# Strassen's seven block products in the second layer of a fused attention and MLP kernel

## The chip, the cores and the metric

The kernel runs on one core of one Trainium2 chip. The metric is device time in microseconds (us), measured around the whole launch. The time before is 336.84 us, the median of 3 runs (336.18 to 337.52). All runs in this document are of the same undisturbed state, "fast". In the profile, PE is TensorE's matmul, PEld its weight load, DVE is VectorE, ACT is ScalarE, POOL is GpSimd, SP is SyncE (SPq its sequencer). PSUM is the memory in which the kernel puts TensorE's results, and a bank is one buffer of it. The granted clock is the share of TensorE's full clock in the clock records of the trace.

## The reference

Sliding-window attention (window 64) on 8 batches, 8 heads, 576 tokens and 64 columns per head, then a layer norm and a two-layer MLP with a residual:

```python
scores = scale * q @ k.T;  scores = where(0 <= i - j < 64, scores, -1e9)
x  = softmax(scores) @ v                    # [8, 576, 512]
xn = (x - mean) / sqrt(var + 1e-6) * g_ln
out = x + relu(xn @ w_ch1) @ w_ch2          # w_ch1 [512, 2048], w_ch2 [2048, 512]
```

## The kernel before

The tokens are taken in nine groups of 512: groups 0 to 7 are tokens 0 to 511 of each batch, group 8 is the last 64 tokens of all eight. While TensorE runs the MLP of group g, the attention of group g+1 is woven in. The MLP is a list of units, and `at(i, f, ...)` puts a piece of other work behind unit i. So this list is the program order, for every engine. The code is shortened, and the remarks behind # are added.

```python
def b_step(g, kb):                       # attention of 128 tokens, then the mean and variance
    ...                                  # 16 matmuls, reciprocal, xn, bn_stats, bn_aggr
    nc.vector.scalar_tensor_tensor(      # z = (x - mean) * g: needs no variance
        out=z, in0=xn, scalar=mvg[g][:, kb, 0:1], in1=gB, op0=ALU.subtract, op1=ALU.mult)

def zt_step(g, kb, eng="act"):           # z transposed by TensorE, copied out by ScalarE
    for kc in range(NKC):
        nc.tensor.transpose(out=ztp[:, kc, :], in_=z[:, 128*kc:128*(kc+1)], identity=ident16)
    nc.scalar.copy(out=zT[g][:, :, 128*kb:128*kb+128], in_=ztp)

def l2(kb, part):                        # layer 2: 64 matmuls of 512 columns for a group
    for hc in range(4 * part, 4 * part + 4):
        nc.tensor.matmul(out=ch[kb], lhsT=hrT[:, hc, 128*kb:128*(kb+1)], rhs=w2s[:, hc, :], ...)
    if part == 3: add_out(kb)

def add_out(kb):                         # 1/sigma is applied here, at the very end
    nc.vector.scalar_tensor_tensor(out=o, in0=ch[kb], scalar=rstd[g][:, kb:kb+1],
                                   in1=xn, op0=ALU.mult, op1=ALU.add)
    nc.sync.dma_start(out=out[...], in_=o)

# groups 2 to 7; units 0-15 are layer 1, units 16-31 layer 2
for j in range(4):
    at(1 + 6*j, s_mm, b, j);  at(2 + 6*j, s_mask, b, j)
    at(7 + 6*j, b_step, b, j);  at(min(13 + 6*j, 29), zt_step, b, j)
at(13, group_stats, g)                   # 1/sigma of group g by Newton steps
```

ReLU lets 1/sigma wait until the output, so no matmul waits for a variance.

The softmax here doesn't subtract the row's maximum and nothing guards it: scores larger than these inputs give would overflow.

## Time and profile before

The page of the kernel before, parts 1, 2 and 4. The first line has busy time, share of the span and instructions of each engine. The two strips have one digit (tenths) for each of 40 slices of the span. The last line is the chain of waits that ended last, by engine.

```profile
PE 322.8 (96%) x2887; PEld 171.9 (51%) x2887; DVE 168.0 (50%) x307; ACT 175.5 (52%) x292; POOL 114.8 (34%) x198
...
PE   7988999999999999999999999999999999999994
...
PEclk9999999999999999999999999999999999999999
...
PE 85%; DVE 4%; SPq 4%; DMA 2%; ACT 1%; issue 1%; POOL 1%; ACTq 0%
```

TensorE is busy 96% of the time at full clock (mean granted clock 1.000). VectorE has half its time free, on average.

Windows of the kernel before, for groups 0, 1, 4 and 8. The columns are start:end and length, busy time (and instructions) of PE, PEld, DVE, ACT and POOL, then the granted TensorE clock, DMA share and GB/s.

```profile
20.40:59.50 39.10, 36.97 (x345) 20.80 (x345) 24.46 (x43) 19.11 (x33) 25.26 (x26) 1.00 0.99 308
59.50:98.20 38.70, 37.34 (x426) 26.26 (x425) 27.34 (x49) 22.44 (x36) 15.53 (x27) 1.00 0.58 155
...
167.90:201.90 34.00, 34.00 (x305) 17.53 (x304) 17.16 (x31) 19.46 (x32) 13.77 (x23) 1.00 0.69 169
301.70:334.60 32.90, 27.90 (x129) 12.41 (x127) 4.17 (x8) 9.55 (x16) 1.58 (x8) 1.00 0.16 40
```

In group 4, PE is busy 34.00 of 34.00 us and DVE half of it. In group 1, DVE is already at 27.34 of 38.70.

The timeline of the kernel before, TensorE: two stretches of 8 matmuls of 256 columns (layer 1 of group 1), and two of layer 2 at 512 columns in group 8. The columns are start, duration, engine, line, operation, output and inputs, shapes, and how many.

```profile
63.73 1.04 PE L377 MATMUL hph_0_3_1063<-zT_827,w1g 128*128 128x256 f16 x8
64.60 1.04 PE L377 MATMUL hph_0_4_1073<-zT_827,w1g 128*128 128x256 f16 x8
...
319.07 3.62 PE L353 MATMUL ch_1_4645<-w2s,hrT_4513 128*128 128x512 f16 x16
322.53 1.67 PE L353 MATMUL ch_2_4666<-w2s,hrT_4513 128*128 128x512 f16 x7
```

From start to start, 8 matmuls of 256 columns take 0.87 us, 109 ns each; 16 of 512 take 3.46 us, 216 ns each. Half the columns is half the time, with a new weight for each matmul (a weight load takes 98 ns).

The same view, VectorE and GpSimd, in layer 2 of group 4:

```profile
191.00 1.50 POOL L117 CAST qk_1_6_1_2954<-qk_1_6_1_2754 128x1024 f16<-128x1024 f32 x1
191.53 1.52 DVE L264 TENSOR_TENSOR pt_3_3010<-pt_3_3010,mask 128x1024 f16<-128x1024 f16 x1
```

The mask takes about 0.68 us without a cast beside it, and 1.52 us here; the cast, usually 1.04 us, took 1.50. So both became longer where they met.

### The profile page before, as it was taken

The numbers are of one execution on the slowest core, as the hardware profiler recorded it, in microseconds if no ns is written. First come the engines' busy times: TensorE is split into PE (matmuls) and PEld (weight loads), VectorE is DVE, ScalarE is ACT, GpSimd is POOL, SyncE is SP. The second block draws the span as 40 slices with busy tenths as digits, with TensorE's granted clock in tenths as the row PEclk, the third lists the DMA queues.
The fourth block names the chain that finished last, engine by engine and source line by source line (L and its number), as shares of the span: only waits on it lengthen the run. The fifth ranks groups of instructions, "written<-read, shape, count | busy, mean of one in ns | idle before, by whom it ended". The sixth has DMA issues, their size and how long they took to land.

```text
span 334.6 us, 6996 instructions
## 1 busy us (share of the span) xinstructions
PE 322.8 (96%) x2887; PEld 171.9 (51%) x2887; DVE 168.0 (50%) x307; ACT 175.5 (52%) x292; POOL 114.8 (34%) x198
## 2 busy tenths in 40 slices
PE   7988999999999999999999999999999999999994
PEld 2556445786554455545545554456445444444441
DVE  1795682777933565286415751767235714241011
ACT  2586515485267644974468356763675157505500
POOL 7577655413800195008400780058004103201000
PEclk9999999999999999999999999999999999999999
DMA  8999999976239557950369188903460155020022
GB/s 194 284 385 258 355 265 297 256 232 123 62 105 309 103 104 187 309 103 34 118 212 216 29 199 255 219 23 97 118 104 2 65 149 72 16 82 33 0 63 63
DMA packets 85410, 51.02 MB, mean 152 GB/s; under 512 B 55713, under 2 KB 76193, under 8 KB 85378
## 3 DMA queue, kind: packets, MB, share of 16 engines
q1 hardware_dynamic: 84736, 48.24, 54.1%
q0 software_dynamic: 640, 2.33, 3.1%
q8 instruction: 22, 0.36, 0.5%
q14 instruction: 10, 0.08, 0.1%
q10 hardware_dynamic: 2, 0.00, 0.0%
HBM read 38.80 MB, written 9.44 MB: 144 GB/s over the span
## 4 chain that ended last, share of the span: by engine, by line
PE 85%; DVE 4%; SPq 4%; DMA 2%; ACT 1%; issue 1%; POOL 1%; ACTq 0%
DMA w1s_126<-in_moe_w_ch_dram 2%; SPq L130 2%; SPq L78 1%; PE ch_2_852 L353 1%; PE ch_2_3635 L353 1%; PE ch_1_4056 L353 1%; PE ch_1_3588 L353 1%; PE ch_2_3076 L353 1%; PE ch_2_2587 L353 1%; PE ch_1_1979 L353 1%; PE ch_1_4421 L353 1%; PE ch_2_4077 L353 1%; PE ch_1_3029 L353 1%; PE ch_1_2540 L353 1%; PE ch_2_2026 L353 1%
## 5 line engine op out<-in xcount | busy, mean ns | idle before, releaser
L341 PEld LDWEIGHTS <-w1g 128*128 128x128 f16 x480 | 44.9, 98 | 53.0 <-issue 2.9
L377 PEld LDWEIGHTS <-w1g 128*128 128x128 f16 x192 | 18.1, 98 | 5.4 <-issue 2.1
L454 PE MATMUL warm<-mbias,ident_99 128*128 128x512 f16 x21 | 8.1, 491 | 2.3 <-DVE mbias L434 2.3
L353 PEld LDWEIGHTS <-hrT_4513 128*128 128x128 f16 x64 | 6.3, 98 | 7.5
L353 PEld LDWEIGHTS <-hrT_3733 128*128 128x128 f16 x64 | 6.0, 98 | 7.0
L353 PEld LDWEIGHTS <-hrT_2685 128*128 128x128 f16 x64 | 6.0, 98 | 6.5
L353 PEld LDWEIGHTS <-hrT_4162 128*128 128x128 f16 x64 | 6.0, 98 | 6.5
L353 PEld LDWEIGHTS <-hrT_1635 128*128 128x128 f16 x64 | 5.9, 97 | 6.5
L353 PEld LDWEIGHTS <-hrT_992 128*128 128x128 f16 x64 | 5.9, 98 | 6.3
L353 PEld LDWEIGHTS <-hrT_2131 128*128 128x128 f16 x64 | 5.9, 98 | 6.3
L353 PEld LDWEIGHTS <-hrT_3181 128*128 128x128 f16 x64 | 5.9, 98 | 6.3
L362 DVE SCALAR_TENSOR_TENSOR osb_0_4641<-ch_0_4624,rstdg_4598,xn_0_2321 128x512 f32<-128x512 f32 x1 | 0.8, 752 | 16.2 <-PE ch_0_4624 L353 16.2
L329 POOL TENSOR_TENSOR rstmp_1863<-rstdg_1862 128x4 f32<-128x4 f32 x2 | 0.8, 386 | 22.5 <-DVE rstdg_1862 L324 22.4
L329 POOL TENSOR_TENSOR rstmp_2913<-rstdg_2912 128x4 f32<-128x4 f32 x2 | 0.8, 386 | 21.2 <-DVE rstdg_2912 L324 21.2
L329 POOL TENSOR_TENSOR rstmp_3948<-rstdg_3947 128x4 f32<-128x4 f32 x2 | 0.8, 386 | 21.2 <-DVE rstdg_3947 L324 21.2
L329 POOL TENSOR_TENSOR rstmp_2426<-rstdg_2425 128x4 f32<-128x4 f32 x2 | 0.8, 388 | 20.6 <-DVE rstdg_2425 L324 20.6
L329 POOL TENSOR_TENSOR rstmp_3475<-rstdg_3474 128x4 f32<-128x4 f32 x2 | 0.8, 388 | 19.7 <-DVE rstdg_3474 L324 19.6
L106 POOL MEMSET vt_4312<- 128x16 f16 x1 | 0.2, 168 | 21.0 <-PE xps_2_4279 L280 21.0
L309 ACT COPY zT_2461<-ztp_3_4492 128x512 f16<-128x512 f16 x1 | 0.6, 587 | 9.2 <-PE ztp_3_4492 L306 9.2
L392 PE MATMUL ch_0_700<-w2s,hrT_495 128*128 128x512 f16 x16 | 4.8, 381 | 0.1
L180 POOL CAST w1g<-w2s 128x1024 f16<-128x1024 f32 x4 | 4.6, 1157 | 1.0 <-DMA w2s<-in_moe_w_ch_dram 1.0
L454 PEld LDWEIGHTS <-ident_99 128*128 128x128 f16 x21 | 2.1, 118 | 5.1 <-issue 3.4
(1267 smaller groups left out, 918.2 us busy)
## 6 DMA issues: line engine op xcount, KB each, us to landing
w2s<-in_moe_w_ch_dram SPq DMA_DIRECT2D x4, 512.0 KB, 10.6
v_0_110<-in_v_dram SPq DMA_DIRECT2D x4, 256.0 KB, 6.1
v_1_442<-in_v_dram SPq DMA_DIRECT2D x4, 256.0 KB, 7.7
v_2_950<-in_v_dram SPq DMA_DIRECT2D x4, 256.0 KB, 7.4
v_3_1339<-in_v_dram SPq DMA_DIRECT2D x4, 256.0 KB, 4.3
v_4_1785<-in_v_dram SPq DMA_DIRECT2D x4, 256.0 KB, 8.4
v_5_2348<-in_v_dram SPq DMA_DIRECT2D x4, 256.0 KB, 6.7
v_6_2835<-in_v_dram SPq DMA_DIRECT2D x4, 256.0 KB, 6.9
```

What stands on the lines that cost most here:

```text
L78: nc.sync.dma_start(out=t[:, :].rearrange("p (h m) -> p h m", h=H), in_=src[b, :, 256 * half:256 * half + 256, :].rearrange("h (p j) d -> ...
L106: nc.gpsimd.memset(vt[:, :, :, D:D + 1], 1.0)
L130: nc.sync.dma_start(out=v32[b][:, c], in_=v[b, :, 128 * c:128 * c + 128, :].rearrange("h s d -> s h d"),)
L180: nc.gpsimd.tensor_copy(out=dst, in_=t)
L309: nc.scalar.copy(out=dst, in_=ztp)
L329: eng.tensor_tensor(out=ab, in0=rs, in1=rs, op=ALU.mult)
L341: nc.tensor.matmul(out=hps, lhsT=w1g[:, kc, 128 * hc:128 * (hc + 1)], rhs=zT[g][:, kc, :], start=(kc == 0), stop=(kc == NKC - 1),)
L353: nc.tensor.matmul(out=ch[kb], lhsT=hrT[:, hc, 128 * kb:128 * (kb + 1)], rhs=w2s[:, hc, :], start=(hc == 0), stop=(hc == NHC - 1),)
L362: nc.vector.scalar_tensor_tensor(out=o, in0=ch[kb], scalar=rstd[g][:, kb:kb + 1], in1=x_norm[(g, kb)][:, :, :].rearrange("p h d -> p (h d) ...
L377: nc.tensor.matmul(out=hps[:, e], lhsT=w1g[:, kc, 128 * hc:128 * (hc + 1)], rhs=zT[g][:, kc, 256 * half:256 * half + 256], start=(kc == 0) ...
L392: nc.tensor.matmul(out=ch[kb], lhsT=hrT[:, hc, 128 * kb:128 * (kb + 1)], rhs=w2s[:, hc, :], start=(hc == 0), stop=(hc == NHC - 1),)
L454: nc.tensor.matmul(out=warm[:, :].rearrange("p (a i) -> p a i", i=64), lhsT=ident16, rhs=mb, start=True, stop=True)
```

## The change

TensorE is the limit, so the change gives it less to do. Layer 2 of a group is the product of h (512 tokens by 2048) and W2 (2048 by 512). Cut both into 2 by 2 blocks, and Strassen's scheme (Winograd's form) needs seven block products in place of eight. The price is sums of blocks: four sums of h in each group (S1 to S4, each in four pieces), four of W2 once (in group 1), and eight additions of products to the output. They go to VectorE, and are called block sums (of h), W2 sums and post-adds below.

Three rearrangements come with it. Products 1, 6 and 7 add up in one PSUM bank (A), and the output is gathered in place on the residual tile xn. For that, 1/sigma can no longer be applied at the end: z is normalised before layer 1, block by block, with 1/sigma from GpSimd's power operation. And g is multiplied into W1 once. The diff is shortened, with remarks added.

```diff
+    def z_step(g, kb):                       # now needs mean and 1/sigma
+        nc.vector.tensor_scalar(out=z, in0=xv, scalar1=mu, scalar2=rstd[g][:, kb:kb + 1],
+                                op0=ALU.subtract, op1=ALU.mult)
+    def r_step(g, kb):                       # (var + EPS) ** -0.5 on GpSimd
+        nc.gpsimd.tensor_scalar(out=ve, in0=mvg[g][:, kb, 1:2], ..., scalar2=EPS, ...)
+        nc.gpsimd.tensor_tensor(out=rstd[g][:, kb:kb + 1], in0=ve, in1=mhalf, op=ALU.pow)
 ...
+        def s_sums(i):                       # behind layer-1 units 3, 7, 11, 15
+            for o, x, y, op in ((1, a21, a22, ALU.add), (2, None, a11, ALU.subtract),
+                                (3, a11, a21, ALU.subtract), (4, a12, 2, ALU.subtract)):
+                nc.vector.tensor_tensor(out=sS[o][:, c, :], in0=x, in1=y, op=op)
 ...
+            which, a, wv = {
+                1: ("A", hv[:, :, 0, 0:256], w2v[:, :, 0, 0, :]),
+                2: ("B", hv[:, :, 1, 0:256], w2v[:, :, 1, 0, :]),
+                6: ("A", sS[2], wT[2]),
+                5: ("C", sS[1], w2v[:, :, 0, 1, :]),
+                7: ("A", sS[3], wT[3]),
+                4: ("B", hv[:, :, 1, 256:512], wT[4]),
+                3: ("C", sS[4], w2v[:, :, 1, 1, :]),
+            }[n]                             # order 1 2 6 5 7 4 3, 16 matmuls of 256 columns each
 ...
+        def post(which, kb0, f):             # eight in a group
+            nc.vector.tensor_tensor(out=xv, in0=bank[which], in1=xv, op=ALU.add)
 ...
+            for i in range(8):               # group 1 only: the sums of W2
+                at(8 + i, w2_sums, i)
 ...
-                at(7 + 6 * j, b_step, b, j)
-                at(min(13 + 6 * j, 29), zt_step, b, j)
+                at((7, 12, 18, 23)[j], b_step, b, j)
+                at((7, 12, 18, 23)[j], r_step, b, j)
+                at((9, 14, 20, 25)[j], z_step, b, j)
+                at((12, 17, 22, 27)[j], zt_step, b, j)
```

Also in the diff: group 0 keeps its ordinary layer 2; group 1 normalises its first two blocks with Newton steps on VectorE, inside group 0; bank C of product 5 is one of the two PSUM banks that the transposes used; the q/k transposes move to other slots.

## The prediction

> **What bounds it now.** TensorE. The page gives PE 96% of a 334.6 us span and the chain of waits 85% PE; the windows by group show PE busy 34.6 of 34.6 us in group 2 and likewise through group 6, granted clock 1.00. DVE averages 50%, but in group 1 (59.5 to 98.6 us) it is busy 27.6 of 39.1 us, and the chain there runs partly through DVE.
>
> **Gain.** In the timeline, back-to-back 128x512 layer-2 matmuls step by 216 ns (8 in 1.73 us) and 128x256 layer-1 matmuls with a new weight each by 109 ns (8 in 0.87 us), so a 98 ns weight load hides even behind half the columns. A group's layer 2 goes from 64 x 216 = 13.8 us to 7 x 16 x 109 = 12.2 us: 1.6 us less, 12.7 us over eight groups (3.8%). All of it lies on the chain.
>
> **Added on DVE, per group.** 16 block sums of 512 fp16 per partition. The 1024-element fp16 mask takes 0.69 us, so I estimate 0.42 us each, 6.7 us. Eight post-adds from PSUM at about 0.70 us replace four output ops of 0.75: +2.6 us. z without g should be cheaper, and the three Newton ops go: about -2 us. DVE goes from about 17 to 24 us of 34. In group 1, eight weight sums of 0.69 us come too, in the same slots.
>
> **What eats the gain.**
> 1. Group 1: the DVE queue between the vB copies and the first post-add is about 17 us, while PE reaches product 6 in about 9. Product 6 accumulates on the bank that the post-add reads, so PE waits: group 1 becomes 4 to 7 us longer.
> 2. Groups 2 to 5: the trace shows DVE ops with two SBUF inputs alternating with GpSimd casts (mask 0.69 us alone, 1.52 us when a 1.04 us cast runs; single-input Newton ops of 0.16 us became 1.0 us). [...] The q/k casts (4 x 1.04 us) now follow the third per-block rstd, just when the last block sums run, at the end of layer 1. The first post-add is then late; product 6 waits an estimated 0 to 3.5 us, about 2 per group, cancelling the 1.6.
> 3. Group 0: Newton for two blocks (about 2 us) precedes the output ops on DVE: about +1. Tail and start: +1 in all.
> 4. Groups 6 to 8 have no such casts and keep the full 1.6 us each.
>
> Sum: 336.8 - 12.7 + 7 + 8 (group 1; groups 2 to 5) + 2 = 341; the schedule looks hand-tuned, so I take 337.
>
> **Predicted: 337 us, 328 to 346. Faster by over 2%: 0.20; within 2%: 0.55; slower: 0.25.**
>
> **Signs.** Right: layer-2 matmuls 128x256 stepping 109 ns; 128x512 DVE sums at 0.42 us alone, above 1 us beside casts; PE idle before products 6 and 7 "released by DVE"; group 1 longer, groups 6 to 8 about 1.5 us shorter; total PE busy down about 10 us but PE idle up. Wrong: PE idle unchanged and about 12 us gone, or a matmul step above 110 ns.
>
> **What would make it wrong.** If the casts land before the block sums or after them, groups 2 to 5 keep 1.6 us each and the time is near 330. If GpSimd's power op takes several us, each z waits and the layer-1 inputs of the next group come late: above 345. If GpSimd's per-row multiply is much slower than its cast (1.04 us per 1024 elements), the start grows by several us.

The 0.70 us of a post-add is an estimate; in the trace before, the attention's output, a 128x512 operation from PSUM too, takes 0.69. "Cheaper" for z without g was an expectation; its median went from 0.75 us (before) to 0.55 (after).

## More of the kernel before

The waits view of the kernel before, two of TensorE's lines. The columns are who waits, for whom, total us, times, longest us.

```profile
PE ch_2_852 L353 <- DVE osb_0_836 L362: 0.3, 1, 0.3
PE ztp_1_846 L306 <- DVE z_1_821 L294: 0.2, 1, 0.2
```

TensorE waits for VectorE almost nowhere in the groups (0.9 us in all, none of it in groups 2 to 8).

## The result, and the profile after

The changed kernel takes 383.04 us (381.91 to 383.37, 4 runs) against 336.51 us (335.97 to 337.52, 4 runs) before. The ratio is 1.137, with a 95% interval of 1.134 to 1.140: slower by 46.5 us, and outside the predicted range. The result is correct. Ratios here are the mean time of one kernel's fast runs over that of the other's of the same rounds, so not quite the ratio of the medians quoted.

The page of the changed kernel, the same lines as before:

```profile
PE 324.5 (85%) x3277; PEld 213.6 (56%) x3277; DVE 247.0 (65%) x464; ACT 177.3 (47%) x292; POOL 125.9 (33%) x194
...
PE   6989949884967986998689879998699899999992
...
PEclk9999969999696999999989998999999999999998
...
PE 48%; DVE 29%; ACT 8%; POOL 5%; issue 4%; DMA 2%; SPq 1%; POOLq 0%; ACTq 0%
```

DVE's busy time went from 168 to 247 us, and its share of the chain from 4 to 29%. And the clock strip has sixes: slices in which TensorE was granted well under full speed, as never before.

Windows of the changed kernel, groups 0, 1, 4 and 8:

```profile
21.70:66.90 45.20, 38.45 (x345) 21.46 (x345) 27.43 (x55) 19.09 (x33) 22.43 (x27) 0.92 0.93 273
66.90:122.50 55.60, 41.11 (x474) 33.40 (x473) 41.29 (x75) 21.82 (x35) 21.25 (x32) 0.88 0.34 88
...
203.20:242.10 38.90, 34.59 (x355) 22.80 (x353) 27.34 (x48) 19.76 (x33) 14.98 (x22) 0.96 0.61 153
347.70:381.10 33.40, 26.21 (x178) 17.11 (x175) 12.13 (x25) 9.55 (x16) 0.00 (x0) 0.95 0.21 64
```

Waits of TensorE in the changed kernel, the three largest:

```profile
PE ztp L332 <- DVE z L314: 25.8, 16, 5.9
PE pA L436 <- DVE xn L443: 8.5, 4, 2.2
PE pC L436 <- ACT qkT L207: 3.5, 3, 1.2
```

The largest is not in layer 2's own work. It is the transposes of the next group's z, 16 waits with 25.8 us: 15.9 in groups 0 and 1, 1.7 to 2.0 in each of groups 2 to 5, and 2.5 in group 6. The wait before product 6 (pA, for the post-add xn) is 8.5 us, four times, once in each of groups 2 to 5. The third is bank C.

The length of each group, from its first layer-1 matmul to that of the next, read from the traces (us). Group 8 ends with its last matmul, and the tail is the rest of the span.

| | start | g0 | g1 | g2 | g3 | g4 | g5 | g6 | g7 | g8 | tail |
|---|---|---|---|---|---|---|---|---|---|---|---|
| before | 20.4 | 39.1 | 38.7 | 34.0 | 35.7 | 34.0 | 35.7 | 32.2 | 31.8 | 27.9 | 5.0 |
| after | 21.7 | 45.2 | 55.6 | 38.4 | 42.3 | 38.9 | 41.2 | 33.4 | 31.0 | 26.2 | 7.1 |
| difference | +1.3 | +6.1 | +16.9 | +4.4 | +6.6 | +4.9 | +5.5 | +1.2 | -0.8 | -1.7 | +2.1 |

**The gain is there.** The timeline of the changed kernel, products 1 and 2 of group 8:

```profile
361.52 1.91 PE L436 MATMUL pA<-w2s,hrT 128*128 128x256 f16 x16
363.27 0.93 PE L436 MATMUL pB<-w2s,hrT 128*128 128x256 f16 x7
```

Sixteen matmuls start within 1.75 us, 109 ns each, and group 8, which has no next group to prepare, is 1.7 us shorter.

**Group 0.** The timeline of the changed kernel, where 1/sigma of group 1's first two blocks is made by Newton steps on values of 128x2. (DVE L314 x2 are both z; the bracket is TensorE's idle time, and what ended it.)

```profile
49.41 1.04 POOL L126 CAST qk<-qk 128x1024 f16<-128x1024 f32 x1 [0.81 <-DMA qk<-in_k_dram]
49.45 1.02 DVE L356 TENSOR_SCALAR rstmp<-rstmp 128x2 f32<-128x2 f32 x1
...
52.40 1.00 DVE L314 TENSOR_SCALAR z<-xn,mvg,rstdg 128x512 f16<-128x512 f32 x2
53.01 0.61 PE L332 MATMUL ztp<-ident,z 128*128 128x128 f16 x4 [5.86 <-DVE z L314]
```

A Newton step takes 0.16 us alone, 1.02 us where it meets a cast. The Newton chain lasted 4.2 us (48.13 to 52.36), z came after it, and TensorE stood idle for 5.86 us.

**Group 1.** The timeline of the changed kernel, VectorE's queue ahead of the z of group 2's first block (left out: three more block sums and a post-add):

```profile
92.14 0.66 DVE L536 TENSOR_TENSOR wT<-w2s,wT 128x1024 f16<-128x1024 f16 x1
92.71 0.69 DVE L273 TENSOR_TENSOR pt<-pt,mask 128x1024 f16<-128x1024 f16 x1
93.31 0.42 DVE L414 TENSOR_TENSOR sS<-hrT 128x512 f16<-128x512 f16 x1
...
94.78 0.68 DVE L536 TENSOR_TENSOR wT<-w2s,wT 128x1024 f16<-128x1024 f16 x1
95.38 0.54 DVE L314 TENSOR_SCALAR z<-xn,mvg,rstdg 128x512 f16<-128x512 f32 x1
...
95.98 0.61 PE L332 MATMUL ztp<-ident,z 128*128 128x128 f16 x4 [5.84 <-DVE z L314]
```

VectorE ran them in program order: sums that TensorE needs much later (0.42 and 0.66 to 0.68 us each here) went ahead of the z that TensorE stood waiting for, 5.84 us in all.

The second long wait of group 1, 3.78 us, has another cause. The timeline of the changed kernel, the z of group 2's last block and the GpSimd cast beside it:

```profile
112.85 1.90 POOL L145 CAST vA<-v 128x2048 f16<-128x2048 f32 x1
112.87 2.61 DVE L314 TENSOR_SCALAR z<-xn,mvg,rstdg 128x512 f16<-128x512 f32 x1 [0.95 <-POOL rstdg L323]
```

VectorE first waited 0.95 us for 1/sigma, and then this z took 2.61 us, where most take 0.54. No sum stands ahead of it. It is the same 2.61 us in e1 and e2, which have no sums; in e6 and e7, where this cast is on ScalarE, it took 0.86 us.

**Group 4.** The timeline of the changed kernel, the end of layer 1 and product 6:

```profile
222.01 4.79 POOL L126 CAST qk<-qk 128x1024 f16<-128x1024 f32 x4
222.29 1.26 DVE L414 TENSOR_TENSOR sS<-hrT 128x512 f16<-128x512 f16 x1
...
225.82 1.25 DVE L414 TENSOR_TENSOR sS<-hrT,sS 128x512 f16<-128x512 f16 x1
227.00 0.68 DVE L443 TENSOR_TENSOR xn<-pA,xn 128x512 f32<-128x512 f32 x1
227.73 1.87 PE L436 MATMUL pA<-wT,sS 128*128 128x256 f16 x8 [2.03 <-DVE xn L443]
```

Each of the last four sums takes about 1.2 us beside GpSimd's casts, and 0.42 us without. The post-add behind them is late, and it is what frees bank A for product 6. These 8 matmuls also took 1.87 us instead of 1.04: half clock (0.51 granted from 228 to 231 us).

So a sum of 0.42 us became 1.14 to 1.26, which is 0.7 to 0.8 us more: most of a cast of 1.04 us, but not a whole one. The casts grew as well: the four took 4.79 us, 1.20 each. What the two engines share, the traces do not show.

**Bank C.** The timeline of the changed kernel, group 2: ScalarE's copy of a q/k transpose, and product 5, which gets that bank:

```profile
149.94 1.01 ACT L207 COPY qkT<-tp 128x1024 f16<-128x1024 f16 x1 [0.36 <-POOL vA L133]
151.00 1.03 PE L436 MATMUL pC<-w2s,sS 128*128 128x256 f16 x8 [1.16 <-ACT qkT L207]
```

**The clock.** By the clock records of the trace, TensorE's clock is halved (0.5) for 27.3 us of the groups: 6.8 us at the wait shown in group 0, 6.8 us at each of two waits in group 1 (5.84 and 3.78 us), and 3.4 us in groups 3 and 4 each. It often begins inside the wait (at 50.02 us in the wait from 47.14 to 53.01), so TensorE is idle for 7.3 of the 27.3 us, and busy at half clock for 20.0; products' matmuls of 256 columns then start 213 ns apart in place of 109. Before, there is none in the groups. (The 0.95 in the window of group 8 lies behind the last matmul.)

The traces show more. The records of half clock last 3.413 or 6.827 us. The starts of the half clock in the changed kernel (50.02, 94.39, 114.87, 189.96 and 227.51 us) lie 13, 6, 22 and 11 times 3.413 us apart: here they stand on one grid of windows of 3.413 us, and not at the beginnings of the gaps. Laid out on the grid of its trace, the idle time of TensorE within one window goes with what followed. In the changed kernel, half clock came on after five windows, with 1.81 to 3.41 us without a matmul; the other windows at full clock between 20 us and the last matmul had at most 1.60. In the nine traces that have half clock before the last matmul (the changed kernel, e1 to e7 and e11 below), it came on after 24 windows from 20 us on; each had at least 1.81 us without a matmul (by the ends that the trace models). No other window at full clock had more than 1.73. (In e7, it followed two gaps of 0.74 and 1.45 us in group 1, with 1.4 us of work between them.) Once halved, the clock stayed so after the 11 windows with 0.77 us idle or more, and came back after the 24 with 0.74 or less. So in these traces about half a window idle (1.81 of 3.413 us), in one gap or in several, was followed by half clock, and a gap that fell across two windows could go without: 2.03 us in group 2 was split into 0.57 and 1.46, and 2.21 in group 5 into 0.90 and 1.31.

### The profile page after: what moved, and what is told of

Its sections match the earlier page's. It is cut to its first block, busy times and chain, and to the rows that moved or that the text cites. A ratio compares the mean times of both kernels' runs of the same rounds, so it can differ in the third digit from the quotient of the medians.

```text
span 381.0 us, 7905 instructions
## 1 busy us (share of the span) xinstructions
PE 324.5 (85%) x3277; PEld 213.6 (56%) x3277; DVE 247.0 (65%) x464; ACT 177.3 (47%) x292; POOL 125.9 (33%) x194
## 3 DMA queue, kind: packets, MB, share of 16 engines
q1 hardware_dynamic: 85056, 48.24, 47.5%
## 4 chain that ended last, share of the span: by engine, by line
PE 48%; DVE 29%; ACT 8%; POOL 5%; issue 4%; DMA 2%; SPq 1%; POOLq 0%; ACTq 0%
PE hps L368 15%; DVE sS L414 8%; PE pC L436 7%; PE pA L436 6%; DVE xn L443 4%; DVE stats L299 4%; DVE xn L297 4%; DVE z L314 4%; PE pB L436 3%; PE tp L216 3%; ACT pt L266 3%; PE hph L479 2%; PE ztp L332 2%; PE ch L494 2%; DMA v<-in_v_dram 2%
## 5 line engine op out<-in xcount | busy, mean ns | idle before, releaser
L368 PE MATMUL hps<-zT,w1g 128*128 128x512 f16 x480 | 110.9, 380 | 0.0
L372 ACT ACTIVATE hrT<-hps 128x512 f16<-128x512 f32 x120 | 71.7, 600 | 33.9 <-PE hps L368 33.3
L436 PEld LDWEIGHTS <-sS 128*128 128x128 f16 x512 | 50.4, 101 | 20.1 <-issue 13.1
L414 DVE TENSOR_TENSOR sS<-hrT 128x512 f16<-128x512 f16 x64 | 34.3, 535 | 27.2 <-ACT hrT L372 27.2
L207 ACT COPY qkT<-tp 128x1024 f16<-128x1024 f16 x26 | 26.2, 1012 | 47.9 <-PE tp L216 45.1
L266 ACT ACTIVATE pt<-sc 128x512 f16<-128x512 f32 x72 | 39.0, 596 | 18.5 <-PE sc L263 18.1
L436 PE MATMUL pA<-wT,sS 128*128 128x256 f16 x256 | 33.5, 284 | 8.5 <-DVE xn L443 8.5
L436 PEld LDWEIGHTS <-hrT 128*128 128x128 f16 x384 | 37.1, 100 | 6.3
L126 POOL CAST qk<-qk 128x1024 f16<-128x1024 f32 x32 | 36.1, 1157 | 5.7 <-DMA qk<-in_k_dram 3.0
L332 PE MATMUL ztp<-ident,z 128*128 128x128 f16 x144 | 15.0, 230 | 26.4 <-DVE z L314 25.8
L436 PE MATMUL pC<-w2s,sS 128*128 128x256 f16 x256 | 34.1, 282 | 3.5 <-ACT qkT L207 3.5
L314 DVE TENSOR_SCALAR z<-xn,mvg,rstdg 128x512 f16<-128x512 f32 x32 | 29.4, 920 | 10.7 <-POOL rstdg L323 10.7
```

What stands on the lines that cost most here:

```text
L126: nc.gpsimd.tensor_copy(out=dst[:, :].rearrange("p (a j) e d -> p a e j d", j=j), in_=t[:, :].rearrange("p (a e j d) -> p a e j d", e=2, j ...
L266: nc.scalar.activation(out=pt[:, par], in_=sc[par], func=AF.Exp, bias=0.0, scale=scale)
L314: nc.vector.tensor_scalar(out=z, in0=xv, scalar1=mu, scalar2=rstd[g][:, kb:kb + 1], op0=ALU.subtract, op1=ALU.mult)
L332: nc.tensor.transpose(out=ztp[:, kc, :], in_=z[:, 128 * kc:128 * (kc + 1)], identity=ident16)
L368: nc.tensor.matmul(out=hps, lhsT=w1g[:, kc, 128 * hc:128 * (hc + 1)], rhs=zT[g][:, kc, :], start=(kc == 0), stop=(kc == NKC - 1),)
L372: nc.scalar.activation(out=hrT[:, hc, :], in_=hps, func=AF.Relu, bias=0.0, scale=1.0)
```

## The experiments

The theory: VectorE's queue is the new limit, because the block sums stand in it ahead of the z and the post-adds that TensorE waits for. Rivals: (a) normalising before layer 1 is what delays z, with or without sums; (b) the longer operations beside GpSimd's casts make VectorE too slow; (c) the sums of W2 in group 1 do most of it; (d) the half clock is the cost, and the waits only its trigger. Kernels are compared by their ratios to the kernel before.

Group lengths of the runs that the argument uses (us, from their traces):

| | g0 | g1 | g2 | g3 | g4 | g5 | g6 | g7 | g8 | tail |
|---|---|---|---|---|---|---|---|---|---|---|
| e1_no_sums | 47.0 | 45.9 | 36.0 | 36.4 | 33.8 | 36.4 | 32.0 | 30.7 | 26.3 | 7.1 |
| e2_plain_l2 | 44.7 | 43.7 | 34.8 | 36.8 | 34.8 | 36.8 | 32.9 | 32.2 | 27.9 | 5.0 |
| e3_casts_act | 47.5 | 56.3 | 37.4 | 38.6 | 35.5 | 38.6 | 33.4 | 31.0 | 26.2 | 7.1 |
| e12_fill6 | 44.5 | 51.0 | 38.4 | 41.2 | 38.4 | 41.2 | 33.4 | 31.0 | 26.2 | 7.2 |
| e5_restore01 | 38.4 | 43.4 | 38.6 | 41.2 | 38.4 | 42.5 | 33.4 | 31.0 | 26.2 | 7.2 |
| e9_v2_plain | 38.5 | 38.1 | 34.1 | 36.1 | 34.0 | 36.1 | 32.3 | 31.5 | 27.9 | 4.4 |
| e10_v3 | 38.0 | 38.1 | 33.7 | 34.5 | 33.6 | 34.5 | 31.2 | 30.1 | 26.2 | 5.4 |

Group 0 is the same program in the changed kernel and in e1 to e4, and lasted 44.7 to 47.5 us: a difference of less than 3 us in group 0 shows nothing.

### e1_no_sums: the seven products without the sums

Wrong result on purpose (relative error 1.12): the sums are not computed, and the products read plain blocks of the same shape.

```diff
         def s_sums(i):
+            return
 ...
-                6: ("A", sS[2], wT[2]),
+                6: ("A", hv[:, :, 1, 0:256], w2v[:, :, 1, 1, :]),   # 5, 7, 4, 3 likewise
 ...
     def w2_sums(k):
+        return
```

> The changed kernel without the DVE block sums and weight sums: the seven products read plain blocks of the same shapes in their place (wrong result on purpose); all products, post-adds and per-block normalisation stay. Theory A (the sums, standing in the DVE queue ahead of z and of the post-adds, make TensorE wait): groups 1 to 5 fall from 55.6, 38.4, 42.3, 38.9 and 41.2 us to about 39, 33.5, 35, 33 and 35; whole about 340 us. Theory B (the per-block normalisation, each z waiting for the rstd of GpSimd, makes TensorE wait): little changes, above 370 us. Theory C (sharing of PSUM banks with the products' accumulators): above 365 us.

Measured: 352.17 us (2 runs) against 336.24, ratio 1.047. So the sums are worth about 30 us: the ratio fell by 0.090 from 1.137, and 0.090 of 336.5 us is 30. By group, after less e1: 9.7 us in group 1, 2.5, 5.9, 5.1 and 4.9 in groups 2 to 5, 1.4 in group 6. TensorE no longer waits before product 6. But e1 is still 16 us slower than before, although it runs all of the shorter layer 2. It met neither theory's time: the sums are the larger part, and not the whole.

### e2_plain_l2: everything but Strassen

Ordinary layer 2, no sums; normalisation before layer 1, in-place sums, g in W1 and the moved slots stay.

```diff
-            for n in (1, 2, 6, 5, 7, 4, 3):
-                for p in range(2):
-                    units.append(lambda n=n, p=p: stage(n, p))
+            for kb in range(4):
+                for part in range(4):
+                    units.append(lambda kb=kb, part=part: l2(kb, part))
```

> The changed kernel with Strassen undone: ordinary layer 2 (64 matmuls of 512 columns), no sums, plain adds on the residual tile; per-block normalisation, g in W1 and the new slots stay. Theory A: near the kernel before plus what groups 0 and the start lost (about 7 us): 340 to 346 us. Theory B: above 365 us, with TensorE still waiting for z of the next group.

Measured: 352.23 us (2 runs), ratio 1.047, result correct; the 340 to 346 of theory A was missed, and B's 365 too. Rival (a) has a share of its own: 16 us with no block sum at all, 5.6 in group 0, 5.0 in group 1, 0.7 to 1.1 in each of groups 2 to 6. TensorE waits for z in groups 0 and 1 most: 3.80 us, and 3.27 us for the z of 2.61 us described above. Its largest wait in e2:

```profile
PE ztp L332 <- DVE z L314: 9.6, 9, 3.8
```

That e1 and e2 take the same time is instructive. e1 has 12.7 us less of matmuls, and loses it again: its waits for z are 13.9 us instead of 9.6 (2.2 of these 4.3 in group 0, which is the same program, so scatter), its bank waits 3.5 us instead of none, its tail is 2.2 us longer, and it has 17.1 us of half clock in its groups instead of 6.8. A likely reading, which no run isolates, is that a shorter layer 2 brings TensorE earlier to a z that is not ready.

### e3_casts_act: the q/k casts of batches 4 to 7 on ScalarE

```diff
-            nc.gpsimd.tensor_copy(
+            f = nc.gpsimd.tensor_copy if b < 4 else nc.scalar.copy
+            f(
```

> The changed kernel with the q and k casts of batches 4 to 7 on ScalarE and not on GpSimd. If the alternation of DVE sums with GpSimd casts is the larger part of what groups 2 to 5 lost, the last block sums fall from 1.2 to 0.42 us each and these four groups lose about 3 us each: about 371 us. If the sums' own volume is what counts, under 1 us each: about 380 us.

Measured: 373.63 us (2 runs), ratio 1.111. Groups 2 to 5 became 1.1, 3.7, 3.4 and 2.6 us shorter, 10.7 us together; the other groups did not gain, and the whole by 9 us. The timeline of e3, the same place in group 4 as above:

```profile
219.89 0.42 DVE L415 TENSOR_TENSOR sS<-hrT 128x512 f16<-128x512 f16 x1
...
221.02 0.42 DVE L415 TENSOR_TENSOR sS<-hrT,sS 128x512 f16<-128x512 f16 x1
221.36 0.68 DVE L444 TENSOR_TENSOR xn<-pA,xn 128x512 f32<-128x512 f32 x1
...
223.13 1.04 PE L437 MATMUL pA<-wT,sS 128*128 128x256 f16 x8
```

No cast, every sum at 0.42 us, and no idle bracket before product 6. Rival (b) is real: the q/k casts of these four batches are 9 to 11 of the 46 us. That is not all that casts cost, since the v casts and those of the earlier batches stayed on GpSimd (the z of 2.61 us in group 1 is there in e3 too). The q/k casts alone are not the main cause.

### e4_g1_plain: ordinary layer 2 in group 1, the sums of W2 after it

```diff
+            if g == 1:
+                for kb in range(4): ...       # ordinary layer 2
 ...
-            for i in range(8):
-                at(8 + i, w2_sums, i)
+            for i in range(8):
+                at(40, w2_sums, i)            # behind the whole of group 1
```

> The changed kernel with ordinary layer 2 in group 1 alone and the weight sums put behind it. Theory A: group 1 falls from 55.6 to about 41 us, group 2 grows by at most 2: about 370 us. Theory B: group 1 stays above 50 us.

Measured: 372.55 us (2 runs), ratio 1.108. Group 1 fell from 55.6 to 43.8 us, group 2 rose from 38.4 to 39.9. Both kinds of sums left group 1 in this run; it doesn't separate the W2 sums (rival c) from the block sums there. It shows that 11.8 us of group 1's 16.9 come with its Strassen part, and that 5 stay without it, as in e2.

### e11_fill and e12_fill6: dummy matmuls in the waits

To see what the half clock costs (rival d), the waits stay and TensorE is kept busy in them. e11 puts dummy transposes in front of the three longest waits; e12 also puts 16 dummy matmuls in front of product 6.

```diff
+        for _ in range({(1, 0): 80, (2, 0): 85, (2, 3): 50}.get((g, kb), 0)):
+            nc.tensor.transpose(out=ztp[:, 0, :], in_=ident16, identity=ident16)
         for kc in range(NKC):
             nc.tensor.transpose(out=ztp[:, kc, :], in_=z[:, 128 * kc:128 * (kc + 1)], ...)
# e12 as well:
+            if n == 6 and p == 0 and 2 <= g <= 5:
+                for _ in range(16):
+                    nc.tensor.matmul(out=d[:, 0, :, :], lhsT=ident16, rhs=ident16, ...)
```

> The changed kernel with dummy 128x128 transposes of the identity put in front of the three z transposes that waited longest (80, 85 and 50 of them, 4.5, 4.8 and 2.8 us at 56 ns, so they should end about 1 us before z arrives in waits of 5.86, 5.84 and 3.78 us). Result stays correct. Theory A, the half clock after these waits costs real time: the half-clock windows of groups 0 and 1 (20.5 us in all) are gone, group 0 is about 3.4 us shorter (45.2 to about 42) and group 1 up to 6.8 us shorter (55.6 to about 49), the time near 374. Theory B, half clock is hidden behind the wait for VectorE: the windows go but groups 0 and 1 shorten by under 2 us together, the time near 381. If the windows stay although no idle gap above 2 us is left, the gaps are not what brings them.

> As e11_fill, and 16 dummy 128x128 matmuls (0.9 us) in front of product 6 in groups 2 to 5, where the waits for the post-add are 2.0 to 2.2 us, so about 1.2 us of idle remains in each. Theory A: the two 3.4 us half-clock windows of groups 3 and 4 go too, those two groups are up to 1.7 us shorter each than in e11_fill, groups 2 and 5 are the same, the clock is 1.00 throughout. Theory B: the windows go and the groups stay within 0.5 us. If the windows move to other groups, gaps of about 1.3 us at the transposes and the bank are enough to bring them.

Measured: e11 376.75 us (4 runs), ratio 1.120; e12 374.21 us (4 runs), ratio 1.113; both correct. About 1 us or more of each wait was left behind the dummies (0.99 to 1.42 us), so they delayed nothing there. In group 0 of e11, 80 transposes of 128 columns, each with its weight load, took 4.63 us, 58 ns each. In e11 the half clock is gone from groups 0 and 1, and group 1 is 4.6 us shorter; the 1.0 of group 0 is within its scatter. It stayed in groups 3 and 4, and a new window of 3.4 us came up in group 2. In e12 none is left in any group. Groups 0 and 1 of e12 in its windows, with the clock in the third column from the end:

```profile
20.00:64.50 44.50, 41.38 (x424) 25.29 (x424) 27.51 (x55) 19.13 (x33) 24.33 (x30) 1.00 0.98 292
64.50:115.50 51.00, 44.04 (x608) 38.47 (x607) 40.90 (x75) 21.82 (x35) 21.48 (x32) 1.00 0.37 94
```

Each result lies between the two theories. From after to e12, groups 0 to 5 lose 6.9 us in sum, and the ratio falls by 0.025, 8.3 us of 336.5 (the start was 1.7 us shorter in e12's profile, which is run to run scatter: the start varies from 20.0 to 21.7 us between kernels with the same start). So 27.3 us of half clock cost some 6 to 8 us (the lower figure without group 0). Half of it would be 13.7, but TensorE was busy for only 20.0 of the 27.3, so 10.0 is what half speed (213 ns a matmul in place of 109) can have cost. Part of the rest came back as other waits: without the half clock, group 4 waited 3.31 us for z in place of 2.00.

Single windows of 3.4 us cost less than the 1.7 us that half speed would, too: removing one shortened group 2 by 1.5 us (from e11 to e12), group 3 by 1.1 and group 4 by 0.5.

### e5_restore01, e6_act, e7_slots: taking the waits away one after the other

These three were made as steps to a better kernel. e5 gives groups 0 and 1 their old form (z without 1/sigma, 1/sigma on the output, ordinary layer 2), and puts six of the eight W2 sums behind units 26 to 31 of group 0 and two behind group 1. Strassen stays in groups 2 to 8.

```diff
-        if g == 0:                                  # in b_step and z_step
+        if g < 2:
 ...
+            for i in range(6):
+                at(26 + i, w2_sums, i)              # in group 0
```

> The changed kernel with groups 0 and 1 as in the kernel before (z not normalised and so not behind the Newton steps, rstd on the output, ordinary layer 2); Strassen in groups 2 to 8; six of the weight sums moved into the idle DVE time at the end of group 0, two behind group 1. If what groups 0 and 1 lost is the wait for normalised z plus the sums, they return to about 39.5 and 40 us (from 45.2 and 55.6): about 361 us, no half-clock windows in them. If it is the heavier start or g in W1, group 0 stays above 43 us.

Measured: 364.82 us (2 runs, 362.62 and 367.02), ratio 1.084. Group 0 is back at 38.4 us, so its extra 6.1 us came from the Newton chain ahead of z, as e2 had indicated. Group 1 is 12.2 us shorter than after, but at 43.4 us it missed the 40 expected: the z of group 2's last block, 2.61 us long, still kept TensorE waiting for 3.27 us. Groups 2 to 6 are as long as in the changed kernel, within 1.4 us.

e6 also moves the q, k and v casts of batches 3 to 7 to ScalarE.

```diff
-            nc.gpsimd.tensor_copy(
+            f = nc.gpsimd.tensor_copy if b < 3 else nc.scalar.copy
+            f(
 ...                                                 # and v: two ScalarE copies for b >= 3
```

> The run before with the q, k and v casts of batches 3 to 7 on ScalarE: DVE alternates with no cast in groups 2 to 5. From the first look at casts on ScalarE (10.7 us in groups 2 to 5): about 351 us, last block sums at 0.42 us, no TensorE gap before product 6.

Measured: 355.68 us (2 runs), ratio 1.057. That is 9 us less (6.7 between the two profiled runs; e5's two runs lie 4.4 us apart). Group 1 gave 3.5 of it, with the z of its last wait at 0.86 us. Yet groups 3 and 5 hardly gain (41.5 and 41.7 us, after 41.2 and 42.5 in e5). The wait before product 6 is gone, but the wait for bank C has grown from 1.2 to 2.6 us in groups 2, 3 and 5: ScalarE, which has to empty the bank, is now busy with casts.

e7 also moves the transposes of z later, keeps the q/k transposes off bank C ahead of product 5, and issues the last stores from two engines.

```diff
-                at((12, 17, 22, 27)[j], zt_step, b, j)
+                at((14, 19, 23, 28)[j], zt_step, b, j)
 ...
+            if n == 2 and p == 1:
+                tbank["n"] = 1
+            elif n == 6:
+                tbank["shared"] = True
 ...
-                    nc.sync.dma_start(out=out[...], in_=...)
+                    (nc.scalar if r else nc.sync).dma_start(out=out[...], in_=...)
```

> The run before with the transposes of z one or two slots later (TensorE waited for z 16 times in the changed kernel), the transposes of q kept off the PSUM bank that product 5 takes two slots later, and the last stores issued from two engines. If these waits are what is left, groups 2 to 6 lose another 1.5 to 3 us each and the tail 2 us: 336 to 342 us. If the sums cost TensorE something else, it stays near 350 us.

Measured: 340.70 us (4 runs), ratio 1.011 (1.007 to 1.015). Every operation is the same as in e6; their places, one bank and the issuing engine of the last stores are worth 15 us. The tail fell from 7.1 to 5.5 us. In the traces, TensorE's wait for z fell from 11.4 to 0.3 us and the one for bank C from 7.8 us to none, while smaller waits came up elsewhere. How the time divides between the later transposes and the bank was not measured apart.

### e8_v2 and e9_v2_plain: what Strassen is worth when nothing waits

e8 moves more slots, among them the v cast by three units. e9 is e8 with ordinary layer 2 everywhere, so it undoes Strassen alone.

```diff
# e8 against e7
-                at((9, 14, 20, 25)[j], z_step, b, j)
-                at((14, 19, 23, 28)[j], zt_step, b, j)
+                at((10, 15, 20, 25)[j], z_step, b, j)
+                at((15, 19, 23, 28)[j], zt_step, b, j)
# e9 against e8
-            if g == 1:                              # ordinary layer 2
+            if True:
```

> The last version with what its own trace showed moved: z and its transposes one slot apart again, the tail block's attention step one slot earlier (TensorE waited 1.4 us for the single attention bank in groups 3 and 5), the v cast behind the q/k evictions on ScalarE, weight sums one slot earlier, the last q/k transpose ahead of the last z transpose. If these are plain queue-order waits: groups 1, 3, 5 and 7 lose 2 to 3, 2, 2 and 1 us, groups 2 and 4 about 1: 329 to 333 us.

> The same schedule with ordinary layer 2 in every group and no sums: what is the seven-product form itself worth once the queues are in order? By the matmul steps alone (1.6 us for each of seven groups) this should be 11 us slower than the run beside it; if post-adds and sums still cost TensorE waits, only 3 to 8 us slower, or even faster.

Measured: e8 332.21 us (4 runs), ratio 0.985 (0.980 to 0.990); e9 336.00 us (4 runs), ratio 0.997 (0.992 to 1.001). So with this schedule Strassen gains 3.8 us. The matmuls alone would give 11 (seven groups, 1.6 us each). In groups 3 and 5, e8 is 0.5 us longer than e9: it still pays for waits there, and its tail is 1.2 us longer. e9 also shows that normalising before layer 1 need not cost anything (here in groups 2 to 8): it is as fast as the kernel before.

### e10_v3: the slots moved once more

```diff
-                at((7, 12, 18, 23)[j], b_step, b, j)
-                at((10, 15, 20, 25)[j], z_step, b, j)
-                at((15, 19, 23, 28)[j], zt_step, b, j)
+                at((5, 12, 18, 23)[j], b_step, b, j)
+                at((8, 15, 20, 25)[j], z_step, b, j)
+                at((12, 19, 23, 28)[j], zt_step, b, j)
 ...
+                at(22, cast_v, n, 0, 2)             # v in two halves
+                at(24, cast_v, n, 2, 4)
```

> The faster version with the rest of its visible TensorE waits moved: first attention block two slots earlier so that its chain stands ahead of the second block sums, q/k transposes at slots 18, 21, 24 and 26, the v cast in two halves at 22 and 24. Groups 3 and 5 have 2.0 us of TensorE gaps left, groups 2 and 4 0.6: if these are queue order alone, 3 to 5 us go: 327 to 330 us. If they are the total load of DVE and ScalarE, the gaps move and the time stays at 331 to 333 us.

Measured: 328.81 us (6 runs, 327.96 to 329.37) against 336.25 (11 runs), ratio 0.977 (0.9745 to 0.9796), correct. It beats both kernels. How much of its 7 us is Strassen's was not measured with these slots; e9 has 0.2 us or less of TensorE waits in each of groups 2 to 8, so an ordinary layer 2 had little left to gain there. The page of e10, the same lines as before:

```profile
PE 312.9 (96%) x3229; PEld 205.1 (63%) x3229; DVE 216.4 (66%) x435; ACT 202.8 (62%) x322; POOL 93.4 (29%) x174
...
PE   7988999999999998999999998999999999999993
...
PEclk9999999999999999999999999999999999999999
```

DVE's share of the span is 66%, much as the changed kernel's 65%, in a shorter span: 216.4 us in place of 247.0, with 112 block sums in place of 128, and 2 of them above 1 us where it was 17. There the time grew by 46 us. Here PE is at 96% again, at full clock, with 9.9 us less to do than before. TensorE's wait for z is down from 25.8 us:

```profile
PE ztp L337 <- DVE z L319: 2.0, 3, 0.9
```

## Why the prediction was wrong, point by point

- **The gain: right.** Predicted 216 against 109 ns a matmul and 1.6 us a group. Measured 109 ns, and 1.7 us in group 8, the one group without work for a next one.
- **The single durations: right.** The block sum was estimated at 0.42 us and took 0.42 us; the post-add at 0.70 and took 0.68; above 1 us beside casts, and it was 1.14 to 1.26. 512 elements more (the W2 sum against the block sum) took 0.69 - 0.42 = 0.27 us, 0.53 ns each.
- **The mechanism of groups 2 to 5: right, as far as it went.** "The first post-add is then late; product 6 waits ... about 2 per group": it waited 2.03 to 2.21 us, four times, the longest single wait of each of these groups, and e3 showed that the casts cause it.
- **The place of the first wait: wrong, and this is the step that failed.** The prediction put VectorE's added time against products 6 and 7 only. The largest wait was for z of the next group, at the transposes: 25.8 us, 15.9 of it in groups 0 and 1. In groups 2 to 5 it is 1.7 to 2.0 us, on top of product 6's 2.03 to 2.21, and bank C and the half clock came as well. So these groups, put at about +0.4 each (2 less 1.6), came to +4.4, +6.6, +4.9 and +5.5; not all of that is accounted for by waits. Outside group 1, VectorE's sums were counted as a load ("about 17 to 24 us of 34", which would fit) and not as positions in a queue that other engines wait on. That a late z would hold up the next group was seen, but only for the case of a slow power operation.
- **Group 1: the same step.** "4 to 7 us longer" became 16.9. TensorE did not get as far as waiting at product 6; it stood at the transposes, 5.84 us (z behind the sums) and later 3.78 us (z behind 1/sigma and beside a cast). e4 and e2 divide it: 11.8 with the sums, 5 without them.
- **Group 0: mis-sized.** Put at +1, measured +6.1. "Newton for two blocks (about 2 us)" took 4.2 us, because single operations met casts, and it was placed ahead of "the output ops" only. It stood ahead of z. e5, without it, has 38.4 us in group 0.
- **Groups 6 to 8: "keep the full 1.6 us each" held for one of three.** Measured +1.2, -0.8 and -1.7. e1 shows the 1.4 us of sums in group 6; TensorE waits 2.45 us for z there, and 1.17 in e1.
- **The bank: missed.** Product 5 takes a bank of the transposes and waits 1.16 us for ScalarE in groups 2, 3 and 5.
- **The clock: missed.** It was no term of the sum. It measured some 6 to 8 us (e12). The prediction noted 1.00 throughout, and did not ask what idle gaps would do to it.
- **Start and tail: +1 predicted.** The tail measured +2.1, eight stores issued by SyncE one after the other in 5.2 us. The start did not grow beyond its scatter.
- **GpSimd's power operation: short, as hoped, but not free.** It took 0.55 us, and the operation before it 0.19 to 0.54. VectorE waited for it 10.7 us in all, 14 times. In group 2, the z that TensorE first waited for (1.28 us) started 1.31 us after its mean and variance were there, and 0.73 of these VectorE stood idle for GpSimd.
- **The last step, from 341 to 337** "because the schedule looks hand-tuned", went the wrong way. A schedule tuned for the old amounts of work says nothing good about new work put into it.

The theory stands in this form: about 30 of the 46 us are the sums in VectorE's queue (e1), 9 to 11 of these only because of the q/k casts beside them (e3), and 16 are the normalisation and the slots that came with it (e2), in which a cast has a share too (the z of 2.61 us in group 1, 0.86 in e6 with this cast on ScalarE). The half clock's 6 to 8 us is a part of both, not a further term. The parts do not add up exactly, since a wait taken away shows the next one behind it; and the matmuls' saving of 12.7 us is inside the difference as well. Open is what the single moves of e7 contribute, and what W2's sums cost apart from the block sums in group 1.

## What to carry to other kernels

Before giving an idle engine more work, list who waits for that engine and at which position of its queue the awaited result stands: with VectorE busy 65 and 66% of the span, Strassen's sums went with a loss of 46 us in one arrangement and with a gain of 7 us in another, in which their slots, the casts' engine and the first two groups had been changed. A busy TensorE that is given less to do can arrive earlier everywhere (the likely reading of e1 against e2, 13.9 us of waits for z in place of 9.6), so the slack of every producer ahead of it must be checked, not only of those in the changed stage. And count idle time of TensorE that adds up to some 1.8 us within one window of 3.4 us as dearer than it looks, because half clock followed it here (24 windows with 1.81 us or more).
